# Single PSUM banks, nine weight groups ahead and three pairs of transposes beside the conv, in a causal conv with a spectral mix

## The chip, the cores and the metric

The kernel runs on one core of a Trainium2 chip. Its engines are TensorE (PE in the profile, with its weight loads as PEld), VectorE (DVE), ScalarE (ACT), GpSimd (POOL) and SyncE (SP, which here only issues stores). Matmul results land in PSUM, which has eight banks of 2 KiB in each of 128 partitions; all else lives in SBUF. The metric is the device time of one execution in microseconds (us); lower is better.

## What is computed

Two stages follow each other. A causal convolution of seven taps runs along the sequence, with one softmax-normalised filter for each of eight groups of 24 channels. On its output `x` a spectral mix multiplies the 64 lowest frequencies with complex matrices, transforms back, adds the result to `x`, and adds the relu of that sum times a channel matrix.

```
x: (8, 3264, 192)   weight: (8, 7)   w_r, w_i: (64, 192, 192)   w_ch: (192, 192)

w   = softmax(weight)                         # over the 7 taps
x   = causal conv of x with w, per channel group
X   = rfft(x, axis=1)
Yr  = einsum('bmd,mde->bme', Xr, w_r) - einsum('bmd,mde->bme', Xi, w_i)   # 64 modes
Yi  = einsum('bmd,mde->bme', Xr, w_i) + einsum('bmd,mde->bme', Xi, w_r)
u   = x + irfft(Yr + 1j * Yi, n=S, axis=1)
out = u + maximum(u @ w_ch, 0)
```

## The kernel before

The eight batches are taken as four pairs `q`; of a pair the sequence is cut into 26 tiles of 128 positions (`NT`), the last of them half full, and six units of four or five tiles (`UNITS`), so there are 24 units. SBUF holds the convolved input of all pairs in `xall` (bf16). The order of the work is the order of the program: the scheduler is off (`manual_schedule`), and the framework adds only the waits that the data need.

**Conv stage** (lines 378 to 391). For each unit, `conv` does matmuls with banded tap matrices into the PSUM tiles `Z[0]` and `Z[1]`, and ACT and DVE copy one half each back into `xall` (L285, L287). `dft_unit` adds the unit before into the pair's spectrum in `Z[2]`, bank 0 (L293, L297). After the last unit of a pair ACT copies the spectrum to `xs` (L300), and in the next two units `xtrans` transposes it for the two batches in `Z[3]`, bank 0 (L306, L308), and DVE copies it into `xt`, which lies in `mixa` (L311). From the third unit on, `some(1, ...)` runs one job of the list `tjobs`.

**Jobs.** The last stage needs the convolved input with channels on partitions: `cm` (channels 0 to 127) and `ct` (128 to 191), made by `cm_bank` (L342) and `ct_bank` (L353). A job transposes up to eight tiles into one PSUM bank, and `copy` evicts it, two of three on DVE (L322), the third on ACT (L320). A pair has eleven jobs, so 44 in all; four more (`g_bank`, L334) transpose the Fourier table `ftab` in place, once no `dft_unit` needs it any more. In the conv stage a ring of two banks serves them, the second banks of `Z[2]` and `Z[3]`; behind it a ring of four, the banks of `Z[0]` and `Z[1]`.

**Mix stage** (lines 538 to 552). The weights come in 16 groups of four modes, each with two loads of 288 KB on POOL's queue (`load_w`, L399), into five buffers in `arena`; the first five groups are loaded ahead, and `load_w(g + NW)` stands behind `mix(g)`, whose buffer it takes. A step `d` takes two groups: `mix(2d)` (L410), two jobs, `mix(2d + 1)`, `mix_copy` on ACT (L416), two jobs, and `mix_trans`: two transposes into bank 0 of `Z[3]`, a copy on DVE (L426), two transposes into bank 1, a copy on ACT (L428). In the last step the products that need only `cm` and `ct` of the first two output items (`both(..., "c")`, L477) stand where the jobs stood.

**Last stage** (lines 553 to 578). `zw_pair` multiplies the mixed spectrum with the channel matrix (L485, L486) and evicts with a scale, batch 0 of the pair on DVE (L490), batch 1 on ACT (L493). Then 51 items of two tiles each go through the four tiles `Z`, each two banks wide: matmuls (L477), relu on ACT in place (L502), one more product, sum with `xall` on DVE (L521, L510) into one of seven buffers in `arena`, and stores on SP's queue. The `zw_pair` of pairs 2 and 3 stand among the items, at places 20 and 30.

PSUM is four tiles of two banks, allocated once:

```
    Z = [psum.tile([P, 2, 512], F32, tag=f"z{i}", name=f"z{i}") for i in range(4)]
    ZB = [z[:, :, :].bitcast(BF16) for z in Z]
    ring = [(2, 1), (3, 1)]                                     # conv stage
    ring[:] = [(0, 0), (0, 1), (1, 0), (1, 1)]                  # mix stage
```

## Time and profile before

| What | us |
|---|---|
| median of three runs | 215.61 |
| the three runs | 215.61, 215.43, 217.83 |
| profiled execution | 215.89 |
| its span in the profile | 214.1 |

| Engine | busy, us | share of the span | instructions |
|---|---|---|---|
| PE | 168.0 | 78% | 2687 |
| PEld | 111.3 | 52% | 2687 |
| DVE | 117.1 | 55% | 178 |
| ACT | 93.8 | 44% | 129 |
| POOL | 66.6 | 31% | 117 |

The span is what the profile sees, from the first instruction to the last; the execution's own time is 1.8 us longer. A busy PE is not a PE at its peak: matmuls are pipelined and their ends modelled, so spacing of starts says more than lengths. In rows of groups or waits, `z` stands for all PSUM tiles, `arena` also for the weight buffers, `mixa` for `xt` and `zw`. A wait `A <- B` is time in which engine A did nothing until an instruction of B ended; a wait for several is put down to the last.

### The profile page before, as it was taken

The page shows a single profiled execution, that of the slowest core. Times are in us where ns is not written, and L with a number is a line of the kernel's source. Part 1 is how long each engine was busy: PE and PEld are TensorE (multiplying, and loading weights), DVE is VectorE, ACT ScalarE, POOL GpSimd, SP SyncE. Part 2 cuts the span into 40 slices and gives each one's busy share as a digit, 9 for nine tenths or more (in the row PEclk, how much of TensorE's full clock was granted, in tenths as well). Part 3 has the DMA queues.
Part 4 walks back from the last instruction along what each step waited for, and adds up shares of the span by engine and source line. Part 5 has one row for each costly group of instructions (what it writes and reads, how often), then busy time and mean ns, then how long its engine had stood idle before and what let it go on. Part 6 is the DMA issues. An engine that isn't in the chain of part 4 may idle for free.

```text
span 214.1 us, 6282 instructions
## 1 busy us (share of the span) xinstructions
PE 168.0 (78%) x2687; PEld 111.3 (52%) x2687; DVE 117.1 (55%) x178; ACT 93.8 (44%) x129; POOL 66.6 (31%) x117
## 2 busy tenths in 40 slices
PE   0068897997988977576776866889999999999950
PEld 0043565665665645454545543446666665666720
DVE  5987556655764752232222211147877676877680
ACT  2077654464364332122032222166665665666520
POOL 7989897686574003324224200000000000000000
PEclk9999999999999996555555555799999999999997
DMA  5999999999999934999999950007999999999886
GB/s 53 154 183 189 183 169 184 191 190 191 190 156 194 206 53 58 165 151 153 150 159 147 141 97 3 0 11 224 319 306 320 323 312 321 300 292 321 278 248 203
DMA packets 63916, 40.08 MB, mean 187 GB/s; under 512 B 29584, under 2 KB 63888, under 8 KB 63888
## 3 DMA queue, kind: packets, MB, share of 16 engines
q0 software_dynamic: 36000, 19.59, 69.5%
q1 hardware_dynamic: 27888, 20.09, 29.3%
q8 instruction: 21, 0.34, 0.6%
q14 instruction: 7, 0.06, 0.1%
HBM read 39.20 MB, written 20.05 MB: 277 GB/s over the span
## 4 chain that ended last, share of the span: by engine, by line
PE 60%; POOL 10%; DMA 9%; DVE 9%; ACT 6%; issue 4%; DVEq 0%; POOLq 0%; ACTq 0%
PE z L477 30%; PE z L342 8%; POOL xall L123 7%; DMA xall<-in_x_dram 6%; PE z L410 5%; PE z L353 4%; PE z L267 4%; PE z L293 4%; DVE cm L322 3%; DMA arena<-in_moe_w_r_dram 2%; PE z L422 2%; PE z L334 2%; ACT ct L320 2%; ACT cm L320 1%; DVE mixa L311 1%
## 5 line engine op out<-in xcount | busy, mean ns | idle before, releaser
L521 DVE TENSOR_TENSOR arena<-z,xall 128x768 f32<-128x768 f32 x50 | 47.6, 957 | 16.4 <-ACT z L502 11.5
L477 PE MATMUL z<-mixa,ftab 64*128 64x384 bf16 (+1 forms) x432 | 51.5, 317 | 1.9 <-ACT mixa L493 0.8
L502 ACT ACTIVATE z<-z 128x768 f32<-128x768 f32 x51 | 40.5, 795 | 22.8 <-PE z L477 22.8
L123 POOL DMA_DIRECT2D xall<-in_x_dram x48 | 38.4, 814 | 8.7 <-DMA xall<-in_x_dram 6.6
L267 PE MATMUL z<-xall,band 64*64 64x192 bf16 (+2 forms) x800 | 27.0, 267 | 14.2 <-ACT band L167 10.8
L477 PE MATMUL z<-wm,cm 64*128 64x192 bf16 x408 | 34.9, 249 | 0.7 <-DVE arena L510 0.3
L287 DVE CAST xall<-z 128x768 bf16<-128x768 f32 (+1 forms) x24 | 24.5, 1022 | 14.2 <-PE z L267 12.7
L285 ACT CAST xall<-z 128x768 bf16<-128x768 f32 (+1 forms) x24 | 20.4, 851 | 21.0 <-PE z L267 19.5
L267 PEld LDWEIGHTS <-band 64*64 64x64 bf16 x800 | 18.0, 110 | 21.0 <-ACT band L167 11.1
L342 PE MATMUL z<-ident,xall 128*128 128x128 bf16 x208 | 21.8, 265 | 7.6 <-DVE cm L322 2.4
L477 PEld LDWEIGHTS <-cm 64*128 64x128 bf16 x408 | 15.8, 95 | 22.2 <-PE z L477 14.8
L477 PE MATMUL z<-wt,ct 64*128 64x192 bf16 x208 | 25.9, 247 | 0.0
L322 DVE COPY cm<-z 128x1024 bf16<-128x1024 bf16 (+1 forms) x21 | 13.3, 634 | 21.5 <-PE z L342 21.5
L342 PEld LDWEIGHTS <-xall 128*128 128x128 bf16 x208 | 17.5, 119 | 13.1 <-issue 10.4
L399 POOL DMA_DIRECT2D arena<-in_moe_w_r_dram x16 | 9.9, 618 | 43.2 <-PE z L410 42.2
L293 PE MATMUL z<-xall,ftab 128*128 128x384 bf16 x100 | 22.0, 347 | 0.3
L477 PEld LDWEIGHTS <-ftab 64*128 64x128 bf16 x432 | 19.5, 94 | 4.5 <-issue 2.9
L353 PE MATMUL z<-ident,xall 128*64 128x128 bf16 x208 | 11.7, 267 | 4.9 <-DVE cm L322 1.6
L353 PEld LDWEIGHTS <-xall 128*64 128x64 bf16 x208 | 9.3, 137 | 8.8 <-issue 8.8
L293 PEld LDWEIGHTS <-ftab 128*128 128x128 bf16 x100 | 8.4, 101 | 7.5 <-issue 2.2
L320 ACT COPY cm<-z 128x1024 bf16<-128x1024 bf16 (+1 forms) x7 | 6.4, 921 | 12.8 <-PE z L342 12.5
L410 PE MATMUL z<-arena,mixa 128*16 128x192 bf16 x192 | 10.8, 357 | 0.7 <-DVE mixa L311 0.7
(82 smaller groups left out, 131.3 us busy)
## 6 DMA issues: line engine op xcount, KB each, us to landing
out_dram<-arena SPq DMA_DIRECT2D x102, 192.0 KB, 3.2
xall<-in_x_dram POOLq DMA_DIRECT2D x24, 192.0 KB, 8.2
arena<-in_moe_w_r_dram POOLq DMA_DIRECT2D x16, 288.0 KB, 4.7
arena<-in_moe_w_i_dram POOLq DMA_DIRECT2D x16, 288.0 KB, 5.6
xall<-in_x_dram POOLq DMA_DIRECT2D x16, 240.0 KB, 7.6
xall<-in_x_dram POOLq DMA_DIRECT2D x8, 144.0 KB, 7.3
xall<-in_x_dram POOLq DMA_DIRECT2D x2, 96.0 KB, 6.9
wm<-in_moe_w_ch_dram POOLq DMA_DIRECT2D x1, 48.0 KB, 6.7
```

Source lines behind the costliest of these rows:

```text
L123: nc.gpsimd.dma_start(out=xall[:, s0:s0 + nf, i, :], in_=src)
L267: mm = nc.tensor.matmul(ov[c], band[r, h, c.start + shift + 64 * (r is UP and c is LO): c.start + shift + 64 * (r is UP and c is LO) + 64] ...
L285: nc.scalar.copy(out=dst, in_=srcv)
L287: nc.vector.tensor_copy(out=dst, in_=srcv)
L293: nc.tensor.matmul(xp, ftab[:, t, :], xall[:, slot(q, t), :, :], start=(t == 0), stop=False, skip_group_check=True)
L322: nc.vector.tensor_copy(out=out, in_=in_)
L342: nc.tensor.transpose(tp[:, P * k:P * k + P], xall[:, slot(q, t), i, 0:P], ident[:])
L353: nc.tensor.transpose(tp[64 * i:64 * i + 64, P * k:P * k + P], xall[:, slot(q, t0 + k), i, P:D], ident[:], tile_position=(0, 64 * i))
L410: nc.tensor.matmul(yp[32 * p4:32 * p4 + 2 * B, :], xt[:, j, :, m], wts[g % NW][:, p4, j, :], start=(j == 0), stop=(j == 2), tile_position= ...
L477: mm = nc.tensor.matmul(zt[:, bank, cols], l, r, start=(begin and k == 0), stop=(end and k == len(lst) - 1), skip_group_check=True)
L502: nc.scalar.activation(out=zt[:, :, 0:2 * D], in_=zt[:, :, 0:2 * D], func=ACT.Relu)
L521: nc.vector.tensor_tensor(out=o[:, :, :], in0=zt[:, :, 0:2 * D], in1=xall[:, s[0]:s[1] + 1:s[1] - s[0], :, :].rearrange("p k i d -> p k (i ...
```

## The change

PSUM is handed out in stages, by pools that open and close. In the conv stage `Z[0]` and `Z[1]` stay two-bank tiles (pool on the left); the other four banks become tiles `low[0]` to `low[3]` (pool on the right): `low[0]` for the spectrum, `low[1]` and `low[2]` for `xtrans`, `low[2:4]` for the ring. Behind the conv stage the left pool is replaced by four single banks for the ring. In the mix stage `low[0]` and `low[1]` take the mixes in turn, `low[2]` and `low[3]` the two halves of `mix_trans`, whose four transposes now come before both copies. Before the last step the left pool becomes two two-bank tiles for items, behind the last step the right pool two more.

`cm` and `ct` become views of one buffer `cc`. The part of the last pair has room for four weight groups (`NL`), so groups 0 to 3 go there, and groups from 4 on take turns in the five buffers of `arena`; nine groups are loaded ahead, and the reload stands behind mixes from 4 on.

In the conv stage every odd unit runs two jobs, so that three pairs' 33 jobs are due there; the last pair's jobs are held back (`upto`) until the mixes of groups 0 to 3 have been issued. The `g_bank` jobs go first: two before the first mix, two in the first step. Later steps have one job at each of their two places.

`zw_batch` and `zw_copy` replace `zw_pair`: pairs 0 and 1 are evicted batch by batch, by DVE and ACT from different tiles, pairs 2 and 3 by a single ACT copy of both batches.

```diff
@@ -49,15 +49,16 @@
-    psum = ctx.enter_context(tc.tile_pool(name="psum", bufs=1, space=PSUM))
...
-    cm = sb("cm", [NQ, 2 * NF + 1, P], BF16)
-    ct = sb("ct", [NQ, NT, P], BF16)
+    CB = 2 * NF + 1 + NT
+    cc = sb("cc", [NQ, CB, P], BF16)
+    cm, ct = cc[:, :, 0:CB - NT, :], cc[:, :, CB - NT:CB, :]
@@ -78,7 +79,14 @@
-    wts = [arena[:, WGB * i:WGB * (i + 1)].rearrange("p (m j e) -> p m j e", m=4, j=3) for i in range(NW)]
+    late = cc[:, NQ - 1, :, :].rearrange("p k s -> p (k s)")
+    NL = CB * P // WGB
+    wts = [a[:, WGB * i:WGB * (i + 1)].rearrange("p (m j e) -> p m j e", m=4, j=3)
+           for a, n in ((late, NL), (arena, NW)) for i in range(n)]
+
+    def wbuf(g):
+        return wts[g] if g < NL else wts[NL + (g - NL) % NW]
@@ -106,10 +114,16 @@
-    Z = [psum.tile([P, 2, 512], F32, tag=f"z{i}", name=f"z{i}") for i in range(4)]
-    ZB = [z[:, :, :].bitcast(BF16) for z in Z]
+    def psum_pool(name, side):
+        stack = ExitStack()
+        return stack, stack.enter_context(tc.tile_pool(name=name, bufs=1, space=PSUM, side=side))
+
+    conv_stack, pp = psum_pool("pconv", "left")
+    Z = [pp.tile([P, 2, 512], F32, tag=f"z{i}", name=f"z{i}") for i in range(2)]
+    low_stack, pp = psum_pool("plow", "right")
+    low = [pp.tile([P, 512], F32, tag=f"low{i}", name=f"low{i}") for i in range(4)]
@@ -287,7 +301,7 @@
-        xp = Z[2][:, 0, 0:2 * D]
+        xp = low[0][:, 0:2 * D]
@@ -300,7 +314,7 @@
-        tp = Z[3][:, bank, 0:3 * P].rearrange("p (j c) -> p j c", j=3)
+        tp = low[1 + bank][:, 0:3 * P].rearrange("p (j c) -> p j c", j=3)
@@ -321,12 +335,12 @@
-    ring = [(2, 1), (3, 1)]
+    ring = low[2:4]
@@ -387,7 +401,7 @@
-                some(1, NT * q + t0 + n)
+                some(1 + k % 2, min(NT * q + t0 + n, NT * (NQ - 1)))
@@ -396,42 +410,46 @@
-    for g in range(NW):
+    for g in range(NL + NW):
         load_w(g)
...
-        load_w(g + NW)
+        if g >= NL:
+            load_w(g + NW)
...
     def mix_trans(d):
+        ets = [low[2 + t][:, :].bitcast(BF16)[:, 0:2 * P].rearrange("p (g k) -> p g k", g=2) for t in range(2)]
         for t in range(2):
-            et = ZB[3][:, t, 0:2 * P].rearrange("p (g k) -> p g k", g=2)
             for g in range(2):
-                nc.tensor.transpose(et[:, g, :], ymix[d % 2][:, g, 64 * t:64 * t + P], ident[:])
+                nc.tensor.transpose(ets[t][:, g, :], ymix[d % 2][:, g, 64 * t:64 * t + P], ident[:])
+        for t in range(2):
...
+    conv_stack.close()
+    ring_stack, pp = psum_pool("pring", "left")
+    ring[:] = [pp.tile([P, 512], F32, tag=f"r{i}", name=f"r{i}") for i in range(4)]
     xtrans(NQ - 1, 0, 0)
     xtrans(NQ - 1, 1, 1)
-    ring[:] = [(0, 0), (0, 1), (1, 0), (1, 1)]
-    tbank[0] = 0
-    tjobs += [(0, g_bank, 8 * k, min(8, NTM - 8 * k)) for k in range((NTM + 7) // 8)]
+    tjobs = [(0, g_bank, 8 * k, min(8, NTM - 8 * k)) for k in range((NTM + 7) // 8)] + tjobs
+    some(2)
@@ -479,18 +497,16 @@
+    def zw_batch(b, zt, k):
+        nc.tensor.matmul(zt[:, k, 0:2 * D], yet[:, 0, :, b], wm[:], start=True, stop=False)
+        nc.tensor.matmul(zt[:, k, 0:2 * D], yet[:, 1, :, b], w1[:], start=False, stop=True)
+
+    def zw_copy(b, n, src, act):
+        dst = zw[:, b:b + n, :, :].rearrange("p b t d -> p b (t d)")
+        if act:
+            nc.scalar.activation(out=dst, in_=src, func=ACT.Copy, scale=ascale[:, 0:1])
+        else:
+            nc.vector.tensor_scalar(out=dst, in0=src, scalar1=ascale[:, 0:1], scalar2=None, op0=ALU.mult)
@@ -533,27 +549,44 @@
     for d in range(NG // 2):
+        last = d == NG // 2 - 1
         mix(2 * d)
...
+        if not last:
+            some(1, NT * (NQ - 1) if 2 * d < NL else NT * NQ)
...
         mix(2 * d + 1)
         mix_copy(d)
-        if d < NG // 2 - 1:
-            some(2 if d < NG // 2 - 2 else 99)
+        if not last:
+            some(1 if d < NG // 2 - 2 else 99, NT * (NQ - 1) if 2 * d + 1 < NL - 1 else NT * NQ)
...
         mix_trans(d)
-    zw_pair(0, Z[2])
-    zw_pair(1, Z[3])
+        if d == NG // 2 - 2:
+            ring_stack.close()
+            stack, pp = psum_pool("pz0", "left")
+            ctx.push(stack)
+            assign({k: pp.tile([P, 2, 512], F32, tag=f"za{k}", name=f"za{k}") for k in (0, 1)})
+    low_stack.close()
+    stack, pp = psum_pool("pz1", "right")
+    ctx.push(stack)
+    assign({k: pp.tile([P, 2, 512], F32, tag=f"zb{k}", name=f"zb{k}") for k in (2, 3)})
+    for q in range(2):
+        for i in range(2):
+            zw_batch(2 * q + i, items[2 + i][1], q)
+            zw_copy(2 * q + i, 1, items[2 + i][1][:, q:q + 1, 0:2 * D], i)
@@ -561,7 +594,9 @@
-                zw_pair(duo, zt)
+                for i in range(2):
+                    zw_batch(2 * duo + i, zt, i)
+                zw_copy(2 * duo, 2, zt[:, :, 0:2 * D], True)
```

## The prediction

> **What bounds the kernel now.** I read the page's slices first, for the stages and the granted clock:

> ```profile
> PEclk9999999999999996555555555799999999999997
> DMA  5999999999999934999999950007999999999886
> ```

> Each digit is one fortieth of 214.1 us. TensorE's granted clock falls to half after some 80 us and comes back near 136 us; the DMA engines go idle for two slices (75 to 83 us), and again from 128 to 144 us. Then busy time by stage (stretch, its length, then PE, PEld, DVE, ACT, POOL, clock, DMA share, GB/s):

> ```profile
> 24.00:78.20 54.20, 49.86 (x1038) 33.73 (x1037) 34.32 (x49) 24.99 (x31) 32.16 (x48) 1.00 1.38 179
> ...
> 80.80:132.40 51.60, 35.98 (x431) 25.73 (x431) 12.61 (x30) 12.38 (x22) 13.56 (x22) 0.51 0.85 127
> 132.40:139.70 7.30, 5.80 (x61) 3.15 (x61) 1.40 (x3) 1.60 (x5) 0.00 (x0) 0.75 0.01 2
> 139.70:214.10 74.40, 65.70 (x1032) 42.17 (x1031) 50.57 (x54) 42.15 (x54) 0.00 (x0) 0.98 0.85 272
> ```

> The conv stage (to 78.2) keeps PE 92% busy at full clock. The mix stage (80.8 to 139.7) is the soft one: half clock, PE 70% busy, DVE and ACT 24%, DMA 127 GB/s. What holds PE there is seen in PE's timeline of one pair of weight groups, 103.73 to 111.83 (start, length, instruction, idle before and releaser):

> ```profile
> 103.73 0.69 PE L410 MATMUL z<-arena,mixa 128*16 128x192 bf16 x12
> 104.35 1.03 PE L342 MATMUL z<-ident,xall 128*128 128x128 bf16 x8
> 106.17 1.06 PE L353 MATMUL z<-ident,xall 128*64 128x128 bf16 x16 [0.78 <-DVE cm L322]
> 107.16 0.69 PE L410 MATMUL z<-arena,mixa 128*16 128x192 bf16 x12
> ...
> 110.41 0.42 PE L422 MATMUL z<-ident,ymix 128*128 128x128 bf16 x2
> 111.52 0.37 PE L422 MATMUL z<-ident,ymix 128*128 128x128 bf16 x2 [0.70 <-DVE yet L426]
> 111.83 0.69 PE L410 MATMUL z<-arena,mixa 128*16 128x192 bf16 x12
> ```

> Every second transpose job waits for the copy of the job before it, though it writes the other bank: both banks belong to one two-bank tile, and the program orders accesses by tile. The pair takes 8.1 us: two mixes at 0.62 (103.73 to 104.35), four jobs at about 0.97 (106.17 to 107.16), about 0.75 for the `ymix` transposes, and 2.2 us of such waits. Mixes never wait for weights; it is the loads that wait for mixes:

> ```profile
> POOL arena L399 <- PE z L410: 42.2, 11, 15.1
> ```

> **The change, step by step.** Banks as tiles of their own, the nine groups ahead and the moved transposes act on different limits, so I follow the end of each stage.

> *Conv stage.* `some(1 + k % 2, ...)` runs 33 jobs there in the place of 22, all of three pairs. Price of a job at full clock, by the spacing of starts:

> ```profile
> 41.59 0.61 PE L342 MATMUL z<-ident,xall 128*128 128x128 bf16 x8
> 42.13 0.96 PE L267 MATMUL z<-xall,band 64*64 64x192 bf16 x32
> ...
> 43.77 0.64 PE L353 MATMUL z<-ident,xall 128*64 128x128 bf16 x16
> 44.34 1.09 PE L267 MATMUL z<-xall,band 64*64 64x192 bf16 x40
> ...
> 46.16 0.39 PE L342 MATMUL z<-ident,xall 128*128 128x128 bf16 x4
> 46.48 1.07 PE L267 MATMUL z<-xall,band 64*64 64x240 bf16 x32
> ```

> Six jobs at 0.54, three at 0.57, two short ones at 0.32: 5.6 us on PE, which has no room, so all of it lengthens the stage. Against it, the same stretch has these PE waits for copies out of the other bank of a shared tile:

> ```profile
> PE z L353 <- ACT xs L300: 1.2, 2, 0.6
> PE z L342 <- DVE mixa L311: 1.0, 2, 0.5
> PE z L342 <- ACT xs L300: 0.6, 1, 0.6
> ...
> PE z L353 <- DVE mixa L311: 0.5, 1, 0.5
> PE z L306 <- ACT cm L320: 0.4, 2, 0.2
> PE z L306 <- ACT ct L320: 0.2, 1, 0.2
> ```

> They sum to 3.9 us and go, since spectrum, ring and `xtrans` get banks of their own. Net +1.7 us (from +0.5, if other waits go too, to +5.6 if none goes). The eleven more copies lie on DVE (34.3 of 54.2 us busy) and ACT (25.0) beside PE and cost nothing, unless an engine's queue delays a conv copy; then PE would wait at the next conv for what is left of one copy.

> *Hand-over to the mix.*

> ```profile
> 77.88 0.33 PE L297 MATMUL z<-xall,ftab 128*128 128x192 bf16 x2
> 79.19 0.56 DVE L311 CAST mixa<-z 128x384 bf16<-128x384 f32 x1 [1.32 <-PE z L308]
> 80.83 0.46 PE L410 MATMUL z<-arena,mixa 128*16 128x192 bf16 x12 [0.65 <-DVE mixa L311]
> ```

> The second `xtrans` now has its own bank, so the two 0.56 us copies run back to back: mix 0 starts 2.16 after the last spectrum matmul (78.2) and not 2.63. It starts near 80.83 + 1.7 - 0.5 = 82.0. Two `g_bank` jobs fill PE meanwhile.

> *Weights.* The first five groups (ten loads of 288.0 KB) move in 61.3 to 76.4:

> ```profile
> 61.30:76.40 15.10, 13.76 (x298) 9.44 (x297) 9.53 (x14) 6.46 (x10) 4.51 (x8) 1.00 1.17 196
> arena<-in_moe_w_r_dram POOLq DMA_DIRECT2D x16, 288.0 KB, 4.7
> 81.60 0.61 POOL L399 DMA_DIRECT2D arena<-in_moe_w_r_dram  x1 [15.11 <-PE z L410]
> 83.00:84.00 1.00, 1.00 (x16) 0.80 (x18) 0.00 (x0) 0.07 (x1) 0.00 (x0) 0.50 0.56 35
> ```

> That is 3.02 us a group. `x` and the queue ahead are untouched, so group k lands at 61.3 + 3.02 (k + 1): group 8 at 88.5, where before the engines stood idle from 76.4. Groups 0 to 3 lie in the last pair's transposed region, so they are consumed without a reload; group 9 may be issued once mix 4 has read its buffer. From the start of a mix (80.83) to the bytes of its reload took some 2.6 us (few bytes in 83 to 84).

> *PE on the way to mix 4.* The mix stage keeps 15 jobs of 26. Two run before mix 0, two in pair 0, one in pair 1, two in each of pairs 2 to 6. Without bank waits a pair with two jobs takes 1.24 + 1.94 + 0.75 = 3.9 us at half clock, with one job 2.95. What is late next in such a pair is the `ymix` copy, under the second job. So at half clock mix 4 starts at 82.0 + 3.9 + 2.95 = 88.9, bytes of group 9 flow at 91.5, DMA has idled 3.0 us, and the last group lands at 61.3 + 48.3 + 3.0 = 112.6. PE alone would be at mix 15 by 88.9 + 5 x 3.9 + 2.0 (mix 14 and the first held product, 132.4 to 134.36 before) = 110.4. At full clock mix 4 comes near 86.7 (an estimate: PE's work halves, the copies between it do not), DMA idles 0.8 us, and the last group lands at 110.4. The weights end both ways: a new bound. I take 112.0, nearer the half clock, since PE must wait for weights from about group 9 on.

> *From mix 15 to the first use of `zw`.*

> ```profile
> 134.36 0.69 PE L410 MATMUL z<-arena,mixa 128*16 128x192 bf16 x12
> 136.90 0.27 PE L422 MATMUL z<-ident,ymix 128*128 128x128 bf16 x2 [0.38 <-DVE yet L426]
> 139.10 1.13 ACT L493 ACTIVATE mixa<-z,ascale 128x384 bf16<-128x384 f32 x2 [1.63 <-DVE mixa L490]
> 139.74 1.30 PE L477 MATMUL z<-mixa,ftab 64*128 64x384 bf16 x8 [0.84 <-ACT mixa L493]
> ```

> 5.38 us before. The 0.38 goes, and about 0.65 goes because the first two `zw` copies no longer share a tile, so DVE and ACT work side by side: 4.35. But PE now comes there after waiting for weights and may be at half clock through the last product, the transposes and eight `zw` matmuls, up to +1.6. I take 5.2, and 0.6 for a cold start behind it (between 0 and 1.8: the clock came back near 136, some 3.6 us after PE's work turned dense at 132.4, and half of that is lost). First use: 112.0 + 5.2 + 0.6 = 117.8, in place of 139.74.

> *Final stage.* Its four tiles are two-bank tiles again, with the same order and stores; 74.4 us stay. The `zw` copies of the later pairs become one ACT copy of 768 in the slot of a missing relu: nothing, bounded by one such copy, 0.6, either way. Opening and closing pools issues no work; the first writers wait for the last readers of the same banks, which the order of the work has finished by then. If one is late it costs what is left of a copy, some 0.6 each.

> **The sum.** 139.74 - 117.8 = 21.9 us less. The profiled execution took 215.89 us (span 214.1): 194.0. The median of the runs is 0.28 lower: 193.7.

> **The rivals.**

> 1. *PE stays at full clock* through the hand-over and the first pairs. For: the stretch before mix 0 is filled by two jobs. Against: before, it was 45% busy, at full clock, and the clock fell right behind it:

> ```profile
> 78.10:81.50 3.40, 1.52 (x31) 1.05 (x30) 1.12 (x2) 0.48 (x1) 0.00 (x0) 1.00 0.00 0
> 14.81 1.81 PE L267 MATMUL z<-xall,band 64*64 64x240 bf16 x32 [1.77 <-ACT xall L285]
> 33.83 1.08 PE L267 MATMUL z<-xall,band 64*64 64x240 bf16 x32
> ```

> Then the weights land at 110.4 and 4.35 follows: first use at 114.8, 24.9 us less, 190.7 against the median.

> [...]

> 2. *The weights are held up.* If the program tracked the merged `cc` buffer as a whole, as it does the PSUM tiles, the four early loads would wait for the last copy into it, near 80 us, and all later loads behind them on POOL's queue. Sixteen groups from about 82: the last at 130.3, first use near 135.3, 4.4 us less: 211.2, on the edge of no difference. Against: the slices of `arena` do not block each other (a load at 81.60 while mixes of other slices go on).

> 3. *Slower: transposes cost the conv stage its clock.* With a third more jobs a spell of the conv stage might fall under what holds the clock. The rows above show the price: the same 32 conv matmuls took 1.81 us early on, at half speed, and 1.08 later; 68% more. A unit of 2.2 us (42.13 to 44.34) with half a job more, 2.5 us, would take 1.7 longer. From thirteen of the twenty units behind the ramp on, the 21.9 us are eaten; from sixteen on the kernel is over 2% slower; with all twenty it takes about 228. For: in the mix stage, where transposes are 4.6 of PE's 5.9 us of work in a pair, half clock held at 70% busy. Against: the conv stage held full clock with a job in every unit and 8% idle, and the change makes it denser.

> [...]

> **How the numbers follow.** The forecast and its near forms (either clock, net conv cost 0.5 to 5.6) 0.81, rival 1 0.12, rival 2 0.04, rival 3 0.03. The bounds: 190.7 with the conv net at +0.5 gives 189.5; 193.7 with nothing gained in the conv stage is 197.6, and with later loads slowed by a tenth (seven groups, 2.1) near 199.7. Range 189.5 to 200.0. About 2% is what a measurement of this kernel can tell from no change: faster 0.93, same 0.04, slower 0.03.

> **What would show it.** Right: conv stage ending near 80 with no PE wait for `xs`, `mixa` or job copies; DMA busy from 61 to about 110 with one short gap; mixes from about 10 on waiting for `arena` loads; PE gaps of 0.7 to 1.1 us behind transposes gone; first use of `zw` near 118. Wrong: half clock in the conv stage; loads into the late region issued behind 70 us; new PE waits at pool borders; a final stage longer than 74.4 us.

## The result, and the profile after

| | median, us | runs |
|---|---|---|
| before, on the same chip | 216.64 | 215.43 to 217.83 (4) |
| after | 192.3 | 191.28 to 193.72 (4) |

The ratio is 0.888, with a 95% interval of 0.880 to 0.897: 11% faster. Ratios here and below leave out runs more than 1.5% above the fastest of their kernel, while medians and ranges hold all runs. 193.7 us was forecast, in a range of 189.5 to 200.0. The profiled execution took 192.1 us with a span of 190.3; the two spans differ by 23.8 us, and the stages say where.

From the page of the changed kernel, the slices of the granted clock and of the DMA engines:

```profile
PEclk9999999999999999999975555999999999999995
DMA  4999999999999999998999900589999997999985
```

Each digit is now 4.76 us. The half clock is down to five slices, 97.5 to 118 us, from about eleven; the DMA engines work through the hand-over between the stages (near 80 us) and have one long hole, near 110 us, behind the last weights. Busy time by stage of the changed kernel (columns as before; the borders are the last matmul of the spectrum, mix 0, mix 15 and the first use of `zw`):

```profile
24.00:78.70 54.70, 54.04 (x1132) 37.20 (x1132) 38.41 (x57) 27.78 (x35) 36.87 (x54) 1.00 1.45 193
78.70:81.16 2.46, 1.84 (x32) 1.39 (x29) 1.38 (x5) 0.48 (x1) 0.00 (x0) 1.00 1.21 209
81.16:109.98 28.82, 18.64 (x336) 12.06 (x336) 7.74 (x20) 9.13 (x19) 8.59 (x14) 0.78 1.10 183
109.98:116.07 6.09, 5.34 (x37) 2.41 (x38) 1.38 (x3) 1.32 (x3) 0.00 (x0) 0.50 0.00 0
116.07:190.30 74.23, 66.12 (x1033) 42.30 (x1032) 49.59 (x53) 42.93 (x54) 0.00 (x0) 0.96 0.85 272
```

The conv stage keeps PE 99% busy at full clock, with eleven more jobs in it. From mix 0 to mix 15 the weights flow at 183 GB/s in place of 122, and the stretch takes 28.8 us in place of 53.5. The same stretch before:

```profile
80.83:134.36 53.53, 37.87 (x457) 26.60 (x457) 12.61 (x30) 12.64 (x23) 13.56 (x22) 0.51 0.82 122
```

PE's timeline of the changed kernel shows both halves of that stretch, dense pairs first, then waits for weights:

```profile
84.67 0.62 PE L356 MATMUL r<-ident,xall 128*128 128x128 bf16 x8
85.34 0.40 PE L437 MATMUL low<-ident,ymix 128*128 128x128 bf16 x4
85.66 0.46 PE L424 MATMUL low<-arena,mixa 128*16 128x192 bf16 x12
86.05 0.62 PE L356 MATMUL r<-ident,xall 128*128 128x128 bf16 x8
...
98.53 0.70 PE L424 MATMUL low<-arena,mixa 128*16 128x192 bf16 x12 [2.03 <-DMA arena<-in_moe_w_i_dram]
99.16 1.06 PE L367 MATMUL r<-ident,xall 128*64 128x128 bf16 x16
...
107.10 0.70 PE L424 MATMUL low<-arena,mixa 128*16 128x192 bf16 x12 [0.90 <-DMA arena<-in_moe_w_i_dram]
109.98 0.69 PE L424 MATMUL low<-arena,mixa 128*16 128x192 bf16 x12 [0.86 <-DMA arena<-in_moe_w_i_dram]
```

85.66 is mix 4, the first on an `arena` buffer. No transpose waits for a copy of another bank any more, and the last two mixes come 2.88 us apart, the time of one group of weights. The waits of PE and of POOL for each other, from the waits view of the changed kernel (total us, how many, the longest):

```profile
POOL arena L413 <- PE low L424: 9.3, 2, 9.0
PE low L424 <- DMA arena<-in_moe_w_i_dram: 8.2, 6, 2.2
```

Loads waited 42.2 us for mixes before and 9.3 now, nearly all in one wait (group 9 for mix 4); mixes, which never waited for weights, now wait 8.2 us for them. Stage by stage, by the starts of the same instructions in both traces:

| Stretch | before | after | difference |
|---|---|---|---|
| to the first conv matmul | 10.79 | 10.27 | -0.52 |
| to the last spectrum matmul | 67.09 | 68.45 | +1.36 |
| to mix 0 | 2.95 | 2.44 | -0.51 |
| to mix 15 | 53.53 | 28.82 | -24.71 |
| to the first use of `zw` | 5.38 | 6.09 | +0.71 |
| to the end of the span | 74.36 | 74.23 | -0.13 |

All of the gain lies between mix 0 and mix 15. The change has three parts and some small ones, and the trace alone doesn't say which of them made it.

### The profile page after: what moved, and what is told of

It reads as the page before. It is cut to its first block, busy times and chain, and to the rows that moved or that the text cites. A ratio compares the mean times of both kernels' runs of the same rounds, so it can differ in the third digit from the quotient of the medians.

```text
span 190.3 us, 6289 instructions
## 1 busy us (share of the span) xinstructions
PE 156.2 (82%) x2687; PEld 101.6 (53%) x2687; DVE 115.2 (61%) x176; ACT 93.8 (49%) x129; POOL 66.2 (35%) x117
## 4 chain that ended last, share of the span: by engine, by line
PE 70%; DMA 10%; DVE 7%; issue 5%; ACT 4%; POOL 1%; DVEq 0%; POOLq 0%; ACTq 0%
PE za L495 18%; PE zb L495 16%; PE z L281 12%; PE low L307 9%; DMA arena<-in_moe_w_i_dram 6%; PE low L356 5%; DMA arena<-in_moe_w_r_dram 4%; PE low L367 3%; DVE arena L175 2%; PE low L424 1%; PE low L320 1%; DVE xall L301 1%; PE zb L501 1%; PE low L437 1%; PE r L348 1%
## 5 line engine op out<-in xcount | busy, mean ns | idle before, releaser
L495 PEld LDWEIGHTS <-cc 64*128 64x128 bf16 x616 | 24.6, 95 | 21.8 <-PE za L495 7.8
L495 PE MATMUL za<-mixa,ftab 64*128 64x384 bf16 (+1 forms) x232 | 33.2, 318 | 0.6 <-ACT za L518 0.4
L495 PE MATMUL zb<-mixa,ftab 64*128 64x384 bf16 x200 | 30.5, 323 | 0.1
L537 DVE TENSOR_TENSOR arena<-za,xall 128x768 f32<-128x768 f32 x25 | 23.8, 957 | 10.1 <-ACT zb L518 3.1
L537 DVE TENSOR_TENSOR arena<-zb,xall 128x768 f32<-128x768 f32 x25 | 23.8, 957 | 7.9 <-ACT za L518 3.9
L518 ACT ACTIVATE za<-za 128x768 f32<-128x768 f32 x26 | 20.7, 795 | 11.8 <-PE za L495 11.7
L518 ACT ACTIVATE zb<-zb 128x768 f32<-128x768 f32 x25 | 19.9, 795 | 11.2 <-PE zb L495 11.2
L307 PE MATMUL low<-xall,ftab 128*128 128x384 bf16 x100 | 22.0, 348 | 0.0
L495 PE MATMUL za<-wm,cc 64*128 64x192 bf16 x208 | 18.2, 253 | 0.5 <-DVE arena L526 0.3
L495 PE MATMUL zb<-wm,cc 64*128 64x192 bf16 x200 | 16.7, 245 | 0.1
## 6 DMA issues: line engine op xcount, KB each, us to landing
arena<-in_moe_w_r_dram POOLq DMA_DIRECT2D x12, 288.0 KB, 10.9
arena<-in_moe_w_i_dram POOLq DMA_DIRECT2D x12, 288.0 KB, 11.2
cc<-in_moe_w_r_dram POOLq DMA_DIRECT2D x4, 288.0 KB, 7.1
cc<-in_moe_w_i_dram POOLq DMA_DIRECT2D x4, 288.0 KB, 7.8
```

The source lines that it names most:

```text
L307: nc.tensor.matmul(xp, ftab[:, t, :], xall[:, slot(q, t), :, :], start=(t == 0), stop=False, skip_group_check=True)
L495: mm = nc.tensor.matmul(zt[:, bank, cols], l, r, start=(begin and k == 0), stop=(end and k == len(lst) - 1), skip_group_check=True)
L518: nc.scalar.activation(out=zt[:, :, 0:2 * D], in_=zt[:, :, 0:2 * D], func=ACT.Relu)
L537: nc.vector.tensor_tensor(out=o[:, :, :], in0=zt[:, :, 0:2 * D], in1=xall[:, s[0]:s[1] + 1:s[1] - s[0], :, :].rearrange("p k i d -> p k (i ...
```

## The experiments

### One part undone, one part alone

Three kernels undo one part of the change each. The cuts, in the order banks, groups ahead, jobs:

```diff
-    low = [pp.tile([P, 512], F32, tag=f"low{i}", name=f"low{i}") for i in range(4)]
+    LT = [pp.tile([P, 2, 512], F32, tag=f"low{i}", name=f"low{i}") for i in range(2)]
+    low = [LT[i][:, k, :] for k in range(2) for i in range(2)]
...
-    ring[:] = [pp.tile([P, 512], F32, tag=f"r{i}", name=f"r{i}") for i in range(4)]
+    RT = [pp.tile([P, 2, 512], F32, tag=f"r{i}", name=f"r{i}") for i in range(2)]
+    ring[:] = [RT[i][:, k, :] for i in range(2) for k in range(2)]
...
+    low[:] = [LT[i][:, k, :] for i in range(2) for k in range(2)]
```

```diff
-        return wts[g] if g < NL else wts[NL + (g - NL) % NW]
+        return wts[NL + g % NW]
...
-    for g in range(NL + NW):
+    for g in range(NW):
...
-        if g >= NL:
-            load_w(g + NW)
+        load_w(g + NW)
```

```diff
-                some(1 + k % 2, min(NT * q + t0 + n, NT * (NQ - 1)))
+                some(1, min(NT * q + t0 + n, NT * (NQ - 1)))
...
-            some(1, NT * (NQ - 1) if 2 * d < NL else NT * NQ)
+            some(2, NT * (NQ - 1) if 2 * d < NL else NT * NQ)
...
-            some(1 if d < NG // 2 - 2 else 99, ...
+            some(2 if d < NG // 2 - 2 else 99, ...
```

Banks undone:

> The changed kernel, but the four low banks and the four ring banks are again halves of two-bank tiles. Theory (the weights end the mix stage, and bank waits matter by making mix 4, and so the reload of its buffer, late): the conv stage ends some 4 us later than the changed kernel's 79, mix 4 comes near 93 in place of 85.7, the DMA engines idle from 87 to about 95.5, the last group lands near 116 in place of 109: about 199 us (197 to 202). Rival (PE has slack in the mix stage once nine groups are ahead, so waits between banks cost nothing there, and only the conv stage's cost shows, hidden by the weights): 192 to 193.5.

Groups ahead undone:

> The changed kernel with five groups fetched ahead, as before the change; the last pair's jobs stay held back at the same places. Theory (the weights end the mix stage): the DMA engines idle from about 75 to mix 0 (81.2) plus some 2.6; eleven groups at 2.87 then land by about 115.4 in place of 108.9: about 199 us (197.5 to 200.5). Rival (PE's own work sets the end, the loads are hidden as they were before the change): 192 to 193.5.

Moved jobs undone:

> The changed kernel with one transpose job in every unit of the conv stage and two at each place of the mix stage, as before the change: 22 jobs in the conv stage and 26 behind it. Theory (the weights end the mix stage, PE has room under them): mix 0 near 76.5, mix 4 between 83.5 and 88, last group landing at 108 to 111: 192 us (190.5 to 194.5), so the moved jobs alone bring next to nothing. Rival (26 jobs at half clock are PE's own limit, 5.9 us a pair): mix 15 near 121, about 204 us.

Two of these cuts together leave one part alone; all three leave the small things. Single banks alone:

> Only the single banks: five groups ahead and the jobs as before the change. Theory (the weights end the mix stage, and bank waits were what kept the loads back before): mix 0 near 76.5, bytes of the first reload near 79.5, eleven groups at 2.87 by about 111: about 194.5 us (192.5 to 198). Rival (four jobs a pair at half clock bound PE even without waits): mix 15 near 121, about 204 us.

Nine groups alone:

> Only the nine groups ahead: two-bank tiles and the jobs as before the change (with the small things of the run named none). If the mix stage is at half clock with bank waits, PE sets the end and the groups ahead bring nothing: 211 to 216 us. If the clock stays full through the hand-over, mix 4 comes near 89 and the weights or PE end at about 113 to 119: 196 to 203 us.

Moved jobs alone:

> Only the moved jobs: two-bank tiles and five groups ahead. Theory (the weights end the mix stage): the conv stage ends near 84 as without single banks, mix 0 near 86.4, first reload's bytes near 89, eleven groups at 2.87 by about 120.6: 204 to 208 us, whatever the clock. Rival (PE still sets the end): over 210 us.

None of the three:

> All three parts undone in the changed kernel: two-bank tiles, five groups ahead, one job a unit in the conv stage and two at each place of the mix stage. What stays is small: two table jobs between the conv stage and mix 0, the four transposes of a pair ahead of both copies, the evictions of zw. If these small things count for nothing: 213 to 217 us, as before the change. Rival (the two table jobs fill the hand-over, the clock stays full there, and a pair then takes some 5.6 us in place of 8.1): mix 15 near 120, 200 to 206 us.

Measured, each against runs of the kernel before on the same chip in the same session (the kernels were run on several chips):

| Kernel | banks | ahead | jobs | median, us | range | ratio, 95% interval |
|---|---|---|---|---|---|---|
| after | x | x | x | 192.3 | 191.28 to 193.72 | 0.888 (0.880 to 0.897) |
| jobs undone | x | x | | 191.78 | 190.89 to 193.99 | 0.889 (0.884 to 0.894) |
| banks undone | | x | x | 198.13 | 197.99 to 198.83 | 0.921 (0.917 to 0.925) |
| ahead undone | x | | x | 200.32 | 199.58 to 202.24 | 0.932 (0.926 to 0.937) |
| banks alone | x | | | 196.48 | 195.26 to 198.62 | 0.911 (0.906 to 0.915) |
| ahead alone | | x | | 200.72 | 197.0 to 206.45 | 0.913 (0.904 to 0.923) |
| jobs alone | | | x | 205.52 | 203.99 to 207.66 | 0.945 (0.939 to 0.951) |
| none | | | | 204.16 | 199.99 to 206.25 | 0.928 (0.917 to 0.939) |

Where the range is wide, ratio and median part: by the medians, ahead alone comes to 0.924 and none to 0.940 of the kernel before (217.25 us there).

Each undone part landed in the range that "the weights end the mix stage" gave it, and so did banks alone and jobs alone; ahead alone landed in the range for a clock that stays full, none in that of its rival. The mechanism shows in the traces. With the banks undone, mix 4 starts at 91.67 us in place of 85.66, and the DMA engines idle in between. With five groups ahead, they idle from 75 us on until mix 0 has read its buffer. From the busy time by stretch of the two kernels (the last column is GB/s), banks undone first:

```profile
88.00:93.00 5.00, 4.10 (x91) 2.81 (x88) 1.41 (x4) 2.68 (x6) 0.56 (x1) 1.00 0.01 3
```

```profile
76.00:78.00 2.00, 2.00 (x54) 1.46 (x57) 1.63 (x2) 0.82 (x2) 0.00 (x0) 1.00 0.00 0
```

The moved jobs brought nothing on top of the other two parts: with 22 jobs in the conv stage and 26 behind it the time is 191.8 against 192.3, well inside the intervals. The conv stage ends 3.3 us earlier (75.42 against 78.72), but the weights still land until past 107 us, and the 26 jobs fit under them. PE's mixes in that kernel, the jobs undone:

```profile
91.29 0.46 PE L424 MATMUL low<-arena,mixa 128*16 128x192 bf16 x12
93.99 0.47 PE L424 MATMUL low<-arena,mixa 128*16 128x192 bf16 x12 [0.74 <-DMA arena<-in_moe_w_i_dram]
97.50 0.69 PE L424 MATMUL low<-arena,mixa 128*16 128x192 bf16 x12 [1.93 <-DMA arena<-in_moe_w_i_dram]
...
108.94 0.69 PE L424 MATMUL low<-arena,mixa 128*16 128x192 bf16 x12 [0.89 <-DMA arena<-in_moe_w_i_dram]
```

Mix 15 comes at 108.94 there, 1.0 us sooner than in the changed kernel. Where only five groups are ahead, moving the jobs costs time. With single banks the median goes from 196.48 us to 200.32, with intervals apart (0.906 to 0.915 and 0.926 to 0.937): mix 0, which sets the first reload free, starts at 82.39 us in place of 77.86, and mix 15 comes 4.4 us later. Jobs alone against none shows the same direction, 0.945 against 0.928, less clearly by the medians (0.946 against 0.940).

The surprise is the last row. With all three parts undone the kernel is still 7% faster than before the change (6% by the medians), and even its longest run, 206.25 us, is 5% below the 217.25 of the kernel before. Most of the 11% is thus there without any of the three named parts.

### The clock

The kernel named none keeps full clock until 106.9 us; the kernel before lost it at 81.5 and had half clock until 136. Three kernels ask what the clock is worth and what holds it. The first takes the two table jobs out of the hand-over; the second adds unread matmuls to the hand-over of the kernel before; the third adds them where the changed kernel waits for weights.

```diff
-    some(2)
...
-            some(1, NT * (NQ - 1) if 2 * d < NL else NT * NQ)
+            some(1 if d else 2, NT * (NQ - 1) if 2 * d < NL else NT * NQ)
...
-            some(1 if d < NG // 2 - 2 else 99, ...
+            some((1 if d else 2) if d < NG // 2 - 2 else 99, ...
```

> The changed kernel without the two table jobs between xtrans and mix 0; they run in the first pair instead. Theory (their filling keeps the clock full, the prediction having bet on half clock): without them the clock falls to half behind mix 0, mix 4 comes near 88 to 89 in place of 85.7, the last group lands 2 to 3 us later: 194 to 196 us. Rival (the dense pairs behind the hand-over keep or regain the clock by themselves): 192 us, no difference.

```diff
+    def spin(n):
+        for _ in range(n):
+            nc.tensor.matmul(Z[0][:, 0, 0:2 * D], ident[:], xall[:, 0, :, :], start=True, stop=True)
...
     dft_unit(*units[-1])
+    spin(3)
...
     xtrans(NQ - 1, 0, 0)
+    spin(3)
     xtrans(NQ - 1, 1, 1)
+    spin(3)
```

> The kernel before the change, with nine matmuls of 384 columns added whose results nobody reads: three in each idle gap of PE between the conv stage and mix 0 (gaps of 0.57, 0.66 and 0.65 us). Theory (the fall of the clock in that hand-over kept the whole mix stage at half speed, and a pair then takes 8.1 us in place of 5 to 6): with the gaps filled the clock stays full, the mix stage is 5 to 10 us shorter: 205 to 211 us. Rival (the mix stage falls to half clock by its own gaps, whatever happens before it): 215 to 217 us.

```diff
+    SPIN = {g: 9 for g in range(10, 16)}
+
+    def spin(g):
+        for _ in range(SPIN.get(g, 0)):
+            nc.tensor.matmul(low[3][:, 0:2 * D], ident[:], xall[:, 0, :, :], start=True, stop=True)
...
+        spin(2 * d)
         mix(2 * d)
...
+        spin(2 * d + 1)
         mix(2 * d + 1)
```

> The changed kernel with nine unread matmuls of 384 columns (about 1.45 us) ahead of each mix from group 10 on, where PE waits for weights. Theory (the half clock costs only the tail behind mix 15, as the prediction had it, +1.6 and a cold start): the clock stays full, mix 15 comes at the same time, the first use of zw 1.5 to 2 us sooner: 190 to 191 us against 192.3. Rival (the last stage waits for its stores, so a warm start does not show): 192 us.

| Kernel | median, us | range | ratio, 95% interval | full clock lost at |
|---|---|---|---|---|
| after, table jobs out of the hand-over | 194.03 | 193.4 to 195.32 | 0.895 (0.890 to 0.901) | 99.2 |
| before, hand-over filled | 212.33 | 211.89 to 213.32 | 0.982 (0.977 to 0.987) | 90.1 |
| after, waits for weights filled | 190.56 | 190.16 to 191.31 | 0.881 (0.876 to 0.885) | not lost |

The first landed in the range of its theory for another reason: its clock stayed full through the first pairs without the table jobs, and mix 0 to mix 4 took 4.4 us, against 4.5 in the changed kernel. Its conv stage, whose code is unchanged, ended 2 us later (80.68) in the profiled run. Most of that is an early stretch of half clock, 24.1 to 27.5 us, where the changed kernel's trace has full clock; first this kernel, then the changed one:

```profile
24.10:27.40 3.30, 3.30 (x42) 2.07 (x35) 1.47 (x3) 0.80 (x1) 3.10 (x9) 0.50 1.46 169
24.10:27.40 3.30, 3.30 (x85) 2.28 (x77) 2.00 (x4) 1.70 (x2) 3.26 (x7) 1.00 1.60 190
```

The same conv matmul near 32 us comes 1.45 us later there. The intervals of the two kernels overlap, so no cost of the table jobs is shown, and in the changed kernel they are not what holds the clock. In the kernel named none that was not tried.

The second gained 4.3 us, less than the theory wanted and more than its rival. The clock held through the hand-over but only for one and a half pairs: from 86.6 to 90.0 us the waits between banks left PE 1.58 us busy of 3.40, and it fell there. Then it came back at 97 and fell again at 100.4. Busy time of that kernel ahead of each turn:

```profile
86.60:90.00 3.40, 1.58 (x29) 1.15 (x27) 0.82 (x2) 1.25 (x2) 1.23 (x2) 1.00 1.18 189
93.60:97.00 3.40, 3.09 (x40) 2.24 (x40) 0.22 (x1) 1.18 (x2) 0.64 (x2) 0.51 1.19 194
97.00:100.40 3.40, 1.61 (x32) 1.24 (x31) 1.49 (x5) 0.65 (x2) 1.84 (x3) 0.99 1.03 151
```

The third shows the worth of the clock in the changed kernel. PE's timeline of it:

```profile
110.64 0.46 PE L424 MATMUL low<-arena,mixa 128*16 128x192 bf16 x12
114.86 1.30 PE L495 MATMUL za<-mixa,ftab 64*128 64x384 bf16 x8
```

Mix 15 to the first use of `zw` takes 4.22 us in place of 6.09. Mix 15 itself is 0.7 us later, since the added matmuls overshoot the wait there, and 1.7 us of 192.3 are gained in all, as the theory had it. By the ratios alone this gain is not clear of noise (0.876 to 0.885 against 0.880 to 0.897).

### Loads that never pause

If the weights end the stage, the hole of the DMA engines between group 8 and group 9 is next. Placing groups 0 to 4 in `arena` and 5 to 8 in the last pair's region lets mix 0, not mix 4, set the first reload free.

```diff
-        return wts[g] if g < NL else wts[NL + (g - NL) % NW]
+        if g < NW:
+            return wts[NL + g]
+        return wts[g - NW] if g < NL + NW else wts[NL + (g - NL) % NW]
...
-        if g >= NL:
-            load_w(g + NW)
+        if g < NW:
+            load_w(g + NL + NW)
+        elif g >= NL + NW:
+            load_w(g + NW)
```

> The changed kernel with groups 0 to 4 in the five buffers of arena and 5 to 8 in the last pair's region, so that the first reload can be issued behind mix 0 and not behind mix 4; the last pair's jobs wait until mix 8 is issued and run two at a place from there. Theory (the weights end the mix stage): the DMA engines do not idle at all between 59 and the last landing, which comes near 105.5 in place of 108.9: about 189 us (188 to 190). Rival (four jobs a pair behind group 8 make PE the limit): 191 to 194 us.

190.82 us (190.46 to 191.66), ratio 0.882 (0.877 to 0.888): above the 188 to 190 expected, and by its interval not yet apart from the changed kernel. The rival does not fit either, for the last mixes still wait for loads. The hole is gone; busy time of the changed kernel, then of this one, and this one's last mix:

```profile
86.00:88.00 2.00, 1.64 (x44) 1.19 (x36) 0.42 (x3) 1.33 (x3) 1.57 (x3) 1.00 0.53 74
86.00:88.00 2.00, 1.21 (x37) 0.73 (x28) 0.23 (x1) 0.84 (x3) 1.76 (x3) 1.00 1.21 206
```

```profile
108.31 0.70 PE L426 MATMUL low<-arena,mixa 128*16 128x192 bf16 x12 [0.85 <-DMA arena<-in_moe_w_i_dram]
```

Mix 15 starts at 108.31 in place of 109.98, 1.7 us sooner. The 105.5 of the expectation came from a start of the weights put at 59; with the 61.3 of the prediction and 2.87 us a group, sixteen groups end at 107.2, and mix 15 follows 1.1 us later. Filling the waits as well, with six or seven matmuls each:

> The kernel of the run arena_first with six or seven unread matmuls of 384 columns ahead of each mix from group 11 on, where PE waits for weights. Theory (the weights end the mix stage and the clock sets the tail behind it, so the two gains add): clock full throughout, mix 15 near 108.3, first use of zw some 4.3 us behind it, near 112.6: 188.5 to 189.5 us. Rival (the last stage is held by something else, such as the first stores, and does not begin earlier): 190.5 to 191 us, as without them.

188.02 us (187.81 to 190.8), ratio 0.869 (0.867 to 0.871): both gains, a little more than expected, clear of the changed kernel's interval, and the best of all kernels run. Mix 15 starts at 108.41 and the first use of `zw` follows at 112.63, 4.22 us later, at full clock throughout.

## Why the prediction was right

**Conv stage.** +1.7 us was the net, 5.6 for the jobs less 3.9 for the waits. The stage ended 0.84 us later (78.72 against 77.88); it was 1.36 longer, since its first matmul came 0.5 sooner. PE's waits for copies of other banks are gone, but the jobs were priced too high. Four kernels whose traces all have 3.4 us of half clock near 25 us can be compared: single banks end the stage 3.8 us sooner (75.41 with banks alone against 79.19 with none), and eleven jobs end it 4.5 us later (79.95 with ahead undone against 75.42 with jobs undone). That DVE and ACT have room for their copies held: no conv matmul waits for them behind 24 us.

**Weights as the new bound.** This step carried the forecast, and held in the changed kernel and in each of the three with one part undone: mixes from group 10 on, or sooner, wait for `arena` loads, and undoing the banks or the groups ahead costs 5.8 and 8.0 us by the medians (by the ratios 3.3 and 4.4%, some 7 and 9 us) by making the loads late. A last landing 7 and 6.5 us later had been worked out beforehand from mix 4 and mix 0; mix 15 came 6.3 and 9.6 us later. It is not a law of all variants: with nine groups alone no mix waits for weights, with none of the parts only the last two do, 1.3 us in all. The group's time was 2.87 us (0.59 MB at the 206 GB/s of steady stretches) where 3.02 had been read from the stretch of mean 196. The hole ahead of group 9 is about 1.5 us where 0.8 to 3.0 had been put.

**Mix 15.** 112.0 was taken and 109.98 came. Two terms of that sum were too large. The price of a group was the greater: sixteen groups at 2.87 us take 45.9 and not 48.3. The other was the hole, some 2.4 us in the forecast and about 1.5 here, for the forecast leaned on half clock in the first pairs, which gives its 112.6 and which the run does not show: full clock held until 97.5, so mix 4 came at 85.66, sooner than the 86.7 of the full-clock form. Against both stands a term put at nothing, the 1.1 to 1.3 us by this reckoning from the end of the last group to mix 15. So the time came out near by errors that partly cancel. Rival 1's condition held in part: the stretch ahead of mix 0 was 75% busy (1.84 of 2.46 us) where 45% had been read before, the clock stayed full through the hand-over, and it fell at 97.5 us, once PE waited for weights (1.02 us busy from 94.2 to 97.6). Its time, 190.7, is what the run with filled waits gave, 190.56; that is partly luck, since mix 15 comes late there (110.64) by the added matmuls and not by the price of a group.

**The tail.** 5.2 us to the first use of `zw` and 0.6 for a cold start were put down; 6.09 came, and of the cold start at most half a microsecond (the last stage took 74.23 us from a cold start, 74.36 before, and 73.7 with filled waits). With mix 15 put 2.0 us too late and the tail 0.3 too short, the forecast lies 1.4 us above the median.

**Rivals 2 and 3.** Loads into the shared `cc` buffer were issued from 57.9 us on, in the conv stage; nothing held them. The conv stage kept its clock with half more jobs, 33 in place of 22 (the prediction calls it a third). That its early matmuls of 1.81 us ran at half speed was the author's estimate: the trace of the kernel before holds clock records only from 23.5 us on. Where half clock is recorded, near 26 us in the kernel without table jobs in the hand-over, eight transposes took 1.06 us, against 0.61 in the changed kernel at full clock.

**What the prediction did not see** is that the mix stage before was slow by a clock that fell at 81.5 us and stayed at half until 136.1, not only by its waits. It priced the pair of 8.1 us by parts at half clock, which is right for that trace, and concluded that the three named parts remove the time. The kernel with none of them runs at 0.928 of the time before; from mix 0 to mix 15 it takes 37.3 us in place of 53.5. What differs there from the kernel before is the order of four transposes ahead of two copies, the table jobs, which come first and two of them in the hand-over, and the evictions of `zw`; its clock stays full to 106.9 us. That the order of the transposes is what keeps the clock full there was not tried apart and is only argued, and the table jobs are a rival left open. The trace of the kernel before with the hand-over filled fits the order. In the 3.4 us ahead of the fall at 90.1 us stands this wait between the two pairs of transposes, which the kernel named none does not have:

```profile
87.77 0.27 PE L427 MATMUL z<-ident,ymix 128*128 128x128 bf16 x2 [0.80 <-DVE yet L431]
```

Without it that stretch would have been some 70% busy (an estimate, 1.58 and 0.80 of 3.40 us) in place of 46.

The prediction's third rival had transposes cost PE its clock, and pointed at the half clock of the mix stage before. The kernel with single banks alone speaks against it: there the clock rose at 95.8 us, behind a stretch that was mostly transposes. Its busy time ahead of that rise:

```profile
92.40:95.80 3.40, 3.40 (x52) 2.36 (x44) 0.82 (x2) 1.76 (x3) 1.73 (x3) 0.50 1.21 206
```

And the same for the instructions on the ring's tiles alone, all of them transposes of jobs and their copies (PE, DVE, ACT):

```profile
92.40:95.80 3.40, 2.03 (x24) 0.69 (x1) 1.01 (x1) 0.50 1.21 206
```

Of 3.40 us, 2.03 were transposes of jobs (another 0.6 those of `ymix`), which leaves some 0.8 for other work, and the clock rose.

## What to carry to other kernels

When a stage is slow for several reasons at once, price the change by what ends the stage next: here weights that land 2.87 us a group, so that what makes a load earlier counts, and eleven jobs moved to another stage brought nothing, or cost 3.8 us where they delayed the first reload. Undo all the named parts together too: here the small things left over held most of the gain. A buffer that is needed late can hold early data, but the place to refill first is the one that is read first. And look at the clock before blaming waits: in the kernel before, 3.40 us in which PE was busy for 1.52 were followed by 54.6 us at half clock, with PE 71% busy in them.

## What the runs showed of the hardware

```profile
96.10:99.50 3.40, 2.00 (x42) 1.56 (x40) 1.56 (x7) 0.78 (x3) 2.27 (x4) 1.00 1.21 207
85.85:89.25 3.40, 1.80 (x40) 1.49 (x40) 1.50 (x3) 1.09 (x2) 0.00 (x0) 1.00 0.10 18
116.25:119.65 3.40, 3.05 (x12) 0.71 (x9) 1.16 (x2) 1.49 (x3) 0.00 (x0) 0.50 0.00 0
```

In the mix stage before, the clock stayed at half from 81.5 to 136.1 us with PE 71% busy (38.88 of 54.60 us), while the kernel named none held full clock with 63% over 27 us. Its busy time over that stretch, in its first 3.4 us and in its last, behind which the clock fell:

```profile
79.50:106.70 27.20, 17.02 (x345) 13.33 (x345) 10.85 (x23) 10.18 (x17) 12.14 (x20) 1.00 0.95 153
79.50:82.90 3.40, 1.84 (x37) 1.52 (x40) 1.62 (x3) 0.52 (x2) 0.00 (x0) 1.00 0.00 0
103.30:106.70 3.40, 1.83 (x42) 1.40 (x40) 1.38 (x2) 1.60 (x3) 2.28 (x4) 1.00 1.21 206
```

Both ends are 54% busy; the clock outlived the one and not the other. Between 53 and 59%, then, both outcomes occur in these traces, and what decides between them this measure does not show.
